# Top-k attention and a cosine FFN on one core: P@V of two units per visit, outputs from ScalarE's queue, decode steps apart, last four units reordered

## The chip, the cores and the metric

The kernel runs on one core of one Trainium2 chip. The metric is the device time of one execution in microseconds (us); lower is better. Before the change the median of 3 runs was 1592.81 us (1592.32 to 1592.93).

A core has five engines with an instruction stream each: TensorE (PE; its weight loads are listed as PEld), VectorE (DVE), ScalarE (ACT), GpSimd (POOL) and SyncE (SP). Each stream runs in order, and an instruction waits for semaphores of other engines or of DMAs. SP only issues DMAs here; a DMA can also be issued from ScalarE's stream.

## The reference

Attention over 8 batches and 8 heads with 576 tokens and 64 dimensions, in which each row keeps its 32 largest scores, followed by a feed-forward network (FFN) over the 4608 tokens:

```python
scores = scale * np.matmul(q, k.transpose(0, 1, 3, 2))
kth = np.partition(scores, -32, axis=-1)[..., -32:-31]
scores = np.where(scores >= kth, scores, -1000000000.0)
scores = scores - np.max(scores, axis=-1, keepdims=True)
attn = np.exp(scores)
attn = attn / (np.sum(attn, axis=-1, keepdims=True) + 1e-09)
x = np.matmul(attn, v)        # then (B,H,S,D) -> (4608, 512)
h = x @ w_in                  # 512 -> 2048
out = (h * np.cos(h)) @ w_out # 2048 -> 512
```

q, k and v are float32. The two weights come as float64 and are read as pairs of 32-bit words; the kernel decodes them to float32.

## The kernel before

**Units and slots.** A unit is 128 tokens of one pair of heads (`hp`); there are 144 units, four for each of 36 blocks of 128 tokens. A loop runs over slots i = 0 to 144. In slot i VectorE does the top-k of unit i: four rounds (`topk_round`, tk0 to tk3) of MAX8 on both heads and, but for the last, MATCH_REPLACE. ScalarE does the mask and the exponentials of unit i-1 (`bounds`, `mask`, `exponentials`; called w). Of unit i-2 (x) VectorE takes the reciprocal of the sums, and GpSimd normalises (`normalise`), splits the words into 16-bit halves (`split`), and SP writes these to DRAM (`write_halves`). For unit i-3 (y) SP issues a transposing DMA that brings the probabilities back as `pT` (`transposes`). For unit i-4 (z) TensorE multiplies `pT` by v (`values`, P@V), and ScalarE copies the result to the block's `xT` (`take_values`). TensorE also computes the scores of unit i+1 in slot i, into the only PSUM tile `sc`, and ScalarE copies them to `s` (`take_scores`). The first eight slots (`early_slot`) and the last four units take a shorter way: TensorE itself transposes (`transposes_now`).

**FFN.** A block with all four units done gets 8 pieces of FF1 (`ff1`, line 380: x @ w_in into PSUM `mm`) and 8 of FF2 (`ff2`, line 456). Between them, per half block (a tile `g` of 1024 columns), ScalarE copies out of PSUM (`take_first`, called by `take_banks`), GpSimd reduces the argument (`reduce_first`, `reduce_second`), ScalarE takes the sine (`sines`, line 437; the sine and the exponential need different tables, so each change costs an ACT_TABLE_LOAD), and GpSimd multiplies (`gate`). The calls `feed(n)` issue up to n pieces; a credit of 4.1 pieces per slot is given out, `ff["tick"]` counts the feeds, and FF2 of a half waits two ticks after its gate. `take_second` copies an output block to `ob` and has SP send it (line 467). After the last slot a loop issues what is left.

**Weights.** 32 chunks of 128 x 512 are loaded in the first slots and decoded in three steps, each on its own engine: `decode_first` (ScalarE, lines 126 to 128), `decode_second` (VectorE, two TENSOR_SCALAR, lines 137 and 138), `decode_third` (GpSimd, two TENSOR_TENSOR, lines 147 and 148). `CHUNKS` bounds the staged chunks and live `g` tiles together.

**Order.** The program fixes the order on every engine: it is that in which the functions `early_slot` and `slot` call the others. SP's stream holds the loads of q, k and v for later batches (`at_slot`), the writes, the transposing DMAs and the outputs, in that order too.

Of the kernel before, what the change touches and what calls it, by code (L numbers as in the profile page):

```python
# [10 lines left out]
F32 = mybir.dt.float32  # L11
# [6 lines left out]
P = 128  # L18
# [13 lines left out]
def kernel(  # L32
# [9 lines left out]
    nc = tc.nc  # L42
# [3 lines left out]
    NT = S // P  # L46
# [83 lines left out]

    def decode_second():


        while wq["second"]:
# [8 lines left out]
    def decode_third(n):  # L143
        for _ in range(min(n, len(wq["third"]))):
            st, w = wq["third"].pop()
# [28 lines left out]
    def load_qk(b, hp):  # L174
        st = pairs.setdefault((b, hp), {})
        also = nc.sync if (b, hp) > (0, 0) else nc.scalar
        t = st["q"] = loads.tile([P, S], F32, tag="q", name="q")
        nc.sync.dma_start(out=t, in_=qT[b, 2 * hp : 2 * hp + 2].rearrange("h d s -> (h d) s"))

        t = st["k"] = loads.tile([P, S], F32, tag="k", name="k")  # L180
        also.dma_start(out=t[0:D], in_=kT[b, 2 * hp])
        nc.sync.dma_start(out=t[D:P, TAIL:S], in_=kT[b, 2 * hp + 1, :, 0:MAIN])
        also.dma_start(out=t[D:P, 0:TAIL], in_=kT[b, 2 * hp + 1, :, MAIN:S])

    def load_v(b, hp):
        st = pairs.setdefault((b, hp), {})
        cols = slice(hp * P, (hp + 1) * P)
        t = loads.tile([P, NT, P], F32, tag="v", name="v", bufs=5)
        nc.sync.dma_start(out=t, in_=v[b, 0:MAIN, cols].rearrange("(c p) e -> p c e", p=P))
# [104 lines left out]
    def transposes(u):  # L294
        rows = u.pop("rows").rearrange("q h k -> (q h) k")
        pT = u["pT"] = work.tile([P, 2 * NT + 1, P], F32, tag="pT", name="pT")
        words = pT.rearrange("p c q -> p (c q)").bitcast(U16)
        nc.sync.dma_start_transpose(
            out=words.rearrange("p (c q) -> p c q", c=2 * NT + 1), in_=rows
        )  # L300

    def transposes_now(u):
# [8 lines left out]
        pT = u["pT"] = work.tile([P, 2 * NT + 1, P], F32, tag="pT", name="pT")  # L311
        for j in range(2):
# [5 lines left out]

    def values(u):

        pT = u.pop("pT")
        o = u["o"] = ps.tile([P, 512], F32, tag="mm", name="o", bufs=4)
        for b, _, rows, r0 in u["parts"]:
            st = pairs[b, u["hp"]]
            r = slice(r0, r0 + rows)
            for c in range(NT + 1):
                for j in range(2):
                    d = slice(j * D, (j + 1) * D)
                    if c < NT:
                        lhsT, rhs = st["v"][:, c, d], pT[:, j * (NT + 1) + c, r]  # L330
                    else:
                        lhsT, rhs = st["v_tail"][:, d], pT[:, NT, r]
                    nc.tensor.matmul(o[d, r], lhsT, rhs, start=c == 0, stop=c == NT)  # L333

    def take_values(u):
        blk = block_of[u["tok"]]
        if "xT" not in blk:
            blk["xT"] = work.tile([P, NP, blk["w"]], F32, tag="xT", name="xT", bufs=5)
        at = u["tok"] - blk["t0"]
        nc.scalar.copy(out=blk["xT"][:, u["hp"], at : at + P], in_=u.pop("o")[:, 0:P])  # L340
        blk["left"] -= 1

# [168 lines left out]
    order = [(b, hp) for b in range(B) for hp in range(NP)]  # L511
    for load, bufs, behind in ((load_qk, 5, -1), (load_v, 5, 4)):
        for n in range(NP, len(order)):
            slot = last[order[n - bufs]] + behind if n >= bufs else NP + 2
            at_slot.setdefault(slot, []).append((load, *order[n]))

# [9 lines left out]
    def early_slot(i, u, w):  # L526
        n = 3 if i < 6 else 2
        if i > 0:
            decode_second()
        topk_round(u, 0)  # L530
        scores(units[i + 1])
        for load, b, hp in at_slot.get(i, []):
            load(b, hp)
        load_weights(n)
        if w:
# [3 lines left out]
            reciprocal(w)  # L539
        topk_round(u, 1)  # L540
        topk_round(u, 2)
        if i == 0:
            decode_second()
        topk_round(u, 3)
        decode_third(1)
        if w:
# [3 lines left out]
        gate(1)  # L550
        decode_third(2)
        feed(2)
# [8 lines left out]
        if w:  # L561
            values(w)
            take_values(w)
        feed(2)
        sines(2)

    def slot(i, u, w, x, y, z):
        now = w and i - 1 >= LAST
        decode_second()
        if x:  # L570
            reciprocal(x)
        if u:
            topk_round(u, 0)
        if w:
            bounds(w)
            mask(w)
            exponentials(w)
        if u:
            topk_round(u, 1)
            topk_round(u, 2)  # L580
        if now:
            reciprocal(w)
        if u:
            topk_round(u, 3)
# [20 lines left out]
        take_banks()  # L605
        decode_third(2)
        decode_first(2)
        if now:
            normalise(w)
        reduce_first()  # L610
        reduce_second()
        feed(2)
        if now:
            transposes_now(w)
            values(w)
            take_values(w)
        feed(1)
        sines(2)

    tt = ps.tile([P, 512], F32, tag="mm", name="warm", bufs=4)  # L620
    for _ in range(8):
        nc.tensor.transpose(tt[:, 0:P], ident, ident)
    load_qk(0, 0)
    load_weights(1)
    load_qk(0, 1)
    load_weights(2)
    scores(units[0])
    take_scores(units[0])
    decode_first(3)
    for i in range(NU + 1):  # L630
# [4 lines left out]
        u, w = (units[i - n] if 0 <= i - n < NU else None for n in range(2))  # L635
        x, y, z = (units[i - n] if EARLY <= i - n < LAST else None for n in range(2, 5))
        if i <= EARLY:
            early_slot(i, u, w)
        else:
            slot(i, u, w, x, y, z)  # L640
    while first or second or full:
# [46 lines left out]
```

## Time and profile before

| | |
|---|---|
| median of 3 runs | 1592.81 us |
| profiled execution: its own time | 1585.37 us |
| profiled execution: span of the instructions | 1583.5 us |
| TensorE busy | 1448.9 us (92%) |
| VectorE busy | 1461.5 us (92%) |
| ScalarE busy | 1155.6 us (73%) |
| GpSimd busy | 1101.0 us (70%) |
| mean share of the DMA engines, queue of SP | 48.6% |
| granted TensorE clock, mean | 0.97 |

All rows below come from one profiled execution. Times are microseconds from the start of its span. Busy time is a union, so two overlapping matmuls count once. In a timeline the number behind the start is how long the group of equal instructions took, and a bracket gives the idle time of the engine before it and what ended that. A wait for several semaphores is put down to the one that came last. A share of busy time over the whole span mixes stages, so the rows are taken stage by stage.

### The profile page before, as it was taken

The page shows a single profiled execution, that of the slowest core. Times are in us where ns is not written, and L with a number is a line of the kernel's source. Part 1 is how long each engine was busy: PE and PEld are TensorE (multiplying, and loading weights), DVE is VectorE, ACT ScalarE, POOL GpSimd, SP SyncE. Part 2 cuts the span into 40 slices and gives each one's busy share as a digit, 9 for nine tenths or more (in the row PEclk, how much of TensorE's full clock was granted, in tenths as well). Part 3 has the DMA queues.
Part 4 walks back from the last instruction along what each step waited for, and adds up shares of the span by engine and source line. Part 5 has one row for each costly group of instructions (what it writes and reads, how often), then busy time and mean ns, then how long its engine had stood idle before and what let it go on. Part 6 is the DMA issues. An engine that isn't in the chain of part 4 may idle for free.

```text
span 1583.5 us, 28533 instructions
## 1 busy us (share of the span) xinstructions
PE 1448.9 (92%) x10356; PEld 1024.1 (65%) x10356; DVE 1461.5 (92%) x3103; ACT 1155.6 (73%) x2244; POOL 1101.0 (70%) x837
## 2 busy tenths in 40 slices
PE   4578778999999999999999999999999999999799
PEld 2466365666666666666666666766666666666575
DVE  7999999999999999999999999999999999999621
ACT  6888756777777777777777777777777777777631
POOL 4688856677777777777777777777777777777500
PEclk9688898999999999999999999999999999999999
DMA  8421454545664456644564446554665446644100
GB/s 270 147 72 51 125 157 133 144 127 151 162 158 127 127 142 165 164 127 141 165 164 127 127 133 174 156 136 125 165 166 134 130 121 155 163 128 130 47 7 14
DMA packets 371596, 212.09 MB, mean 134 GB/s; under 512 B 321280, under 2 KB 337664, under 8 KB 371456
## 3 DMA queue, kind: packets, MB, share of 16 engines
q1 hardware_dynamic: 371296, 210.12, 48.6%
q8 instruction: 81, 1.33, 0.3%
q14 instruction: 59, 0.48, 0.1%
q10 hardware_dynamic: 160, 0.16, 0.0%
HBM read 45.09 MB, written 87.29 MB: 84 GB/s over the span
## 4 chain that ended last, share of the span: by engine, by line
PE 66%; ACT 18%; DVE 9%; DMA 3%; SPq 1%; issue 1%; POOL 0%; ACTq 0%; POOLq 0%; DVEq 0%
PE mm L380 29%; PE o L456 19%; PE o L333 9%; PE sc L206 8%; DVE m L230 4%; DVE rest L233 3%; ACT s L261 3%; DMA pT<-rows 3%; ACT s L253 3%; ACT L437 2%; ACT L261 2%; ACT x L437 2%; ACT s L216 2%; ACT ob L465 1%; ACT nd L244 1%
## 5 line engine op out<-in xcount | busy, mean ns | idle before, releaser
L380 PEld LDWEIGHTS mm<-xT,w_in 128*128 128x128 f32 x4608 | 546.2, 193 | 130.7 <-issue 91.8
L230 DVE MAX8 m<-rest 128x8 f32<-128x576 f32 x864 | 609.6, 747 | 0.0
L380 PE MATMUL mm<-xT,w_in 128*128 128x128 f32 x4608 | 572.3, 279 | 33.1 <-ACT xT L340 33.1
L456 PE MATMUL o<-w_out,g 128*128 128x512 f32 x1152 | 535.9, 598 | 7.3 <-POOL w_out L148 7.0
L233 DVE MATCH_REPLACE8 rest<-m,rest 128x576 f32<-128x576 f32 x576 | 423.6, 743 | 0.0
L287 POOL COPY halves<-s 128x2304 uint16<-128x2304 uint16 x132 | 277.5, 2102 | 176.7 <-DMA rows<-halves 172.3
L456 PEld LDWEIGHTS o<-w_out,g 128*128 128x128 f32 x1152 | 203.3, 191 | 198.5 <-issue 187.9
L275 POOL TENSOR_SCALAR s<-s,rden 128x576 f32<-128x576 f32 x288 | 211.8, 747 | 44.3 <-DVE rden L270 44.1
L230 DVE MAX8 m<-s 128x8 f32<-128x576 f32 x288 | 203.2, 747 | 39.7 <-ACT s L216 39.6
L261 ACT ACTIVATE s<-s,nd 128x576 f32<-128x576 f32 x288 | 219.7, 764 | 0.8
L333 PEld LDWEIGHTS o<-pT,v 128*64 128x64 f32 x2560 | 136.9, 141 | 123.1 <-ACT s L253 42.6
L216 ACT COPY s<-sc 128x1152 f32<-128x1152 f32 x144 | 161.4, 1121 | 71.4 <-PE sc L206 70.5
L233 DVE MATCH_REPLACE8 rest<-m,s 128x576 f32<-128x576 f32 x288 | 211.7, 743 | 0.0
L333 PE MATMUL o<-pT,v 128*64 128x128 f32 (+1 forms) x2560 | 173.3, 276 | 37.4 <-DMA pT<-rows 27.2
L253 ACT ACTIVATE s<-s,nb 128x576 f32<-128x576 f32 x288 | 205.3, 760 | 0.0
L392 ACT ACTIVATE g<-mm 128x512 f32<-128x512 f32 x144 | 85.6, 596 | 159.1 <-PE mm L380 158.9
L206 PE MATMUL sc<-k,q 64*128 64x288 f32 (+1 forms) x1280 | 188.9, 443 | 10.1 <-ACT s L216 6.1
L444 POOL TENSOR_TENSOR g<-g,x 128x1024 f32<-128x1024 f32 x67 | 158.9, 2372 | 14.8 <-ACT x L437 14.8
L427 POOL TENSOR_TENSOR x<-g,x 128x1024 f32<-128x1024 f32 x68 | 161.2, 2370 | 5.7
L418 POOL TENSOR_SCALAR x<-g 128x1024 f32<-128x1024 f32 x68 | 71.3, 1049 | 128.5 <-ACT g L392 119.5
L206 PEld LDWEIGHTS sc<-k,q 64*128 64x128 f32 (+1 forms) x1280 | 102.1, 183 | 54.7 <-issue 20.5
L340 ACT COPY xT<-o 128x128 f32<-128x128 f32 x144 | 37.2, 258 | 100.7 <-PE o L333 100.7
(48 smaller groups left out, 1078.7 us busy)
## 6 DMA issues: line engine op xcount, KB each, us to landing
rows<-halves SPq DMA_DIRECT2D x132, 576.0 KB, 3.3
q<-in_q_dram SPq DMA_DIRECT2D x32, 288.0 KB, 3.2
out_dram<-ob SPq DMA_DIRECT2D x36, 256.0 KB, 2.3
st<-in_moe_w_in_dram SPq DMA_DIRECT2D x16, 512.0 KB, 6.3
v<-in_v_dram SPq DMA_DIRECT2D x32, 256.0 KB, 2.9
st<-in_moe_w_out_dram SPq DMA_DIRECT2D x16, 512.0 KB, 3.5
k<-in_k_dram SPq DMA_DIRECT2D x31, 144.0 KB, 3.4
k<-in_k_dram SPq DMA_DIRECT2D x32, 128.0 KB, 3.6
```

Source lines behind the costliest of these rows:

```text
L206: nc.tensor.matmul(sc[r0 : r0 + rows, j, h, 0:HS], st["q"][d, q0 : q0 + rows], st["k"][d, h * HS : (h + 1) * HS], start=True, stop=True,)
L216: nc.scalar.copy(out=s.rearrange("p j (h w) -> p (j h) w", h=2), in_=u.pop("sc").rearrange("p j h w -> p (j h) w")[:, :, 0:HS],)
L230: nc.vector.max(m8[:, j, at], src[:, j])
L233: nc.vector.match_replace(rest[:, j], m8[:, j, at], src[:, j], NEG)
L253: nc.scalar.activation(out=s[:, j], in_=s[:, j], func=AF.Prelu, bias=nb[:, j, 1:2], scale=SCALE, alpha=FAR)
L261: nc.scalar.activation(out=s[:, j], in_=s[:, j], func=AF.Exp, bias=nd[:, j : j + 1], scale=1.0, accum_out=den[:, j : j + 1],)
L275: nc.gpsimd.tensor_scalar(out=s[:, j], in0=s[:, j], scalar1=rden[:, j : j + 1], scalar2=1.0, op0=ALU.mult, op1=ALU.mult,)
L287: nc.gpsimd.tensor_copy(out=halves, in_=s.rearrange("p (k h) -> p h k", h=2))
L333: nc.tensor.matmul(o[d, r], lhsT, rhs, start=c == 0, stop=c == NT)
L380: nc.tensor.matmul(mm[:, at : at + w], w_in[f // FC][:, c, (f % FC) * P : (f % FC + 1) * P], blk["xT"][:, c], start=c == 0, stop=c == NC - 1,)
L427: nc.gpsimd.tensor_tensor(out=x, in0=g, in1=x, op=ALU.subtract)
L456: nc.tensor.matmul(o, g[:, at : at + P], w_out[f], start=f == 0, stop=f == NF - 1)
```

## The change

P@V: `values` and `take_values` now take a list of units. In odd slots the units i-5 and i-4 are multiplied one after the other into one PSUM bank, and one copy of 128 x 256 takes both to `xT`; in even slots there is no P@V. To hold the older unit a slot longer, `pT` has 3 buffers (2 before) and v has 6 (5 before); `CHUNKS` falls from 9 to 8. FF1 of a block may begin only two ticks after its last copy. The output DMA is issued from ScalarE's stream. `decode_second` stands behind the first top-k round and takes a number; `decode_third` takes all that is ready, behind `normalise`. The last four units get their own function. At the start the loads of q and k of the first unit are split differently.

```diff
-    CHUNKS, XB = 9, 4
+    CHUNKS, XB = 8, 4
...
     def load_qk(b, hp):
...
+        also = nc.sync
+        if (b, hp) == (0, 0):
+            also = nc.scalar
+            also.dma_start(out=q[:, 0:P], in_=qs[:, 0:P])
+        else:
+            nc.sync.dma_start(out=q, in_=qs)
+        also.dma_start(out=k[0:D], in_=kT[b, 2 * hp])
+        nc.sync.dma_start(out=k[D:P, TAIL:S], in_=kT[b, 2 * hp + 1, :, 0:MAIN])
+        nc.sync.dma_start(out=k[D:P, 0:TAIL], in_=kT[b, 2 * hp + 1, :, MAIN:S])
+        if (b, hp) == (0, 0):
+            nc.sync.dma_start(out=q[:, P:S], in_=qs[:, P:S])
...
-    def take_values(u):
-        blk = block_of[u["tok"]]
+    def take_values(us):
+        blk, hp, n = block_of[us[0]["tok"]], us[0]["hp"], len(us)
...
+        nc.scalar.copy(
+            out=blk["xT"][:, hp : hp + n].rearrange("p h q -> p (h q)"),
+            in_=us[0].pop("o")[:, 0 : n * P],
+        )
+        blk["left"] -= n
+        blk["tick"] = ff["tick"]
...
-        nc.sync.dma_start(out=out[row : row + P, :], in_=ob)
+        nc.scalar.dma_start(out=out[row : row + P, :], in_=ob)
...
-        if blk["left"] or wq["ready"] < (((i + 1) * (256 // blk["w"]) - 1) // FC + 1) * NC:
+        if blk["left"] or ff["tick"] < blk["tick"] + 2 or wq["ready"] < (((i + 1) * (256 // blk["w"]) - 1) // FC + 1) * NC:
...
     def early_slot(i, u, w):
         n = 3 if i < 6 else 2
-        if i > 0:
-            decode_second()
         topk_round(u, 0)
+        decode_second(1 if i == 0 else n)
         scores(units[i + 1])
...
     def slot(i, u, w, x, y, z):
-        now = w and i - 1 >= LAST
-        decode_second()
         if x:
             reciprocal(x)
         if u:
             topk_round(u, 0)
+            decode_second(2)
...
-        decode_third(2)
+        decode_third()
         decode_first(2)
-        if now:
-            normalise(w)
         reduce_first()
         reduce_second()
+        feed(3)
+        sines(2)
+
+    def last_slot(i, u, w, x, y, z):
+        if x:
+            reciprocal(x)
+        if u:
+            topk_round(u, 0)
+            topk_round(u, 1)
+        bounds(w)
+        mask(w)
+        exponentials(w)
+        take_banks()
+        sines(1)
+        if z:
+            values(z)
...
+        reciprocal(w)
+        normalise(w)
+        if u:
+            topk_round(u, 2)
+            topk_round(u, 3)
+        gate(2)
         feed(2)
-        if now:
-            transposes_now(w)
-            values(w)
-            take_values(w)
+        transposes_now(w)
+        take_banks()
+        reduce_first()
+        reduce_second()
         feed(1)
-        sines(2)
+        values([w])
+        take_values([w])
+        feed(2)
...
-        x, y, z = (units[i - n] if EARLY <= i - n < LAST else None for n in range(2, 5))
+        x, y = (units[i - n] if EARLY <= i - n < LAST else None for n in range(2, 4))
+        z = units[i - 5 : i - 3] if i % 2 and EARLY <= i - 5 < LAST else None
```

**TensorE's order, slot 83.** Here a block is complete and FF1 of it begins. The names: `o<-pT,v` is P@V, `sc` the scores, `w_in` marks FF1 and `w_out` FF2; the numbers behind `v_tail` belong to the head pairs. Before:

```order
L456 MATMUL o_7179<-w_out_104,g 128x512
L456 MATMUL o_7179<-w_out_105,g 128x512
L333 MATMUL o<-pT,v 64x128 x8
L333 MATMUL o<-pT,v_tail_112 64x128 x2
L206 MATMUL sc<-k,q 128x288 x4
L380 MATMUL mm<-xT,w_in_86 128x128 x16
```

In the changed kernel, at the same place:

```order
L469 MATMUL o_7111<-w_out_104,g 128x512
L469 MATMUL o_7111<-w_out_105,g 128x512
L343 MATMUL o<-pT,v 64x128 x8
L343 MATMUL o<-pT,v_tail_110 64x128 x2
L343 MATMUL o<-pT,v 64x128 x8
L343 MATMUL o<-pT,v_tail_112 64x128 x2
L213 MATMUL sc<-k,q 128x288 x4
L393 MATMUL mm<-xT,w_in_86 128x128 x16
```

Two units' P@V now stand together, and the slot before has none. FF1 of the new block still follows directly on one group of scores.

**ScalarE's order around a sine, an output and a copy of xT.** `x<-x,halfpi` is the sine, `nb`, `nd`, `s` and `den` belong to the exponentials, `ob` is an output block. Before:

```order
L437 ACT_TABLE_LOAD
L437 ACTIVATE x<-x,halfpi 128x1024
L241 ACTIVATE nb<-m_7033 128x4
L244 ACTIVATE nd<-m_7033,nb 128x1 x2
L253 ACTIVATE s<-s,nb 128x576 x2
L261 ACT_TABLE_LOAD
L261 ACTIVATE s,den<-s,nd 128x576 x2
L266 ACTIVATE den<-den,eps 128x2
L465 ACTIVATE ob<-o_6846 128x512
L340 COPY xT<-o 128x128
L216 COPY s<-sc 128x1152
```

In the changed kernel, in the half of the blocks that still have a sine just ahead (the program has 104 table loads in all, 132 before):

```order
L450 ACT_TABLE_LOAD
L450 ACTIVATE x<-x,halfpi 128x1024
L248 ACTIVATE nb<-m_6974 128x4
L251 ACTIVATE nd<-m_6974,nb 128x1 x2
L260 ACTIVATE s<-s,nb 128x576 x2
L268 ACT_TABLE_LOAD
L268 ACTIVATE s,den<-s,nd 128x576 x2
L273 ACTIVATE den<-den,eps 128x2
L478 ACTIVATE ob<-o_6869 128x512
L480 DMA out_dram<-ob 128x512
L349 COPY xT<-o 128x256
L223 COPY s<-sc 128x1152
```

The output's DMA is new in this stream, and the copy of xT is twice as wide. In the other blocks two sines follow one table load a slot after the copy.

**VectorE's order where slots 6 and 7 meet.** `m<-s` is the first MAX8 of a unit, `w_out` the decode. Before:

```order
L137 TENSOR_SCALAR w_out_95<-w_out_95 128x512
L138 TENSOR_SCALAR w_out_95<-w_out_95 128x512
L137 TENSOR_SCALAR w_out_96<-w_out_96 128x512
L138 TENSOR_SCALAR w_out_96<-w_out_96 128x512
L230 MAX m_884<-s 128x8 x2
L233 MATCH_REPLACE rest<-m_884,s 128x576 x2
L270 RECIPROCAL rden<-den 128x2
```

In the changed kernel:

```order
L237 MAX m_881<-s 128x8 x2
L240 MATCH_REPLACE rest<-m_881,s 128x576 x2
L137 TENSOR_SCALAR w_out_94<-w_out_94 128x512
L138 TENSOR_SCALAR w_out_94<-w_out_94 128x512
L137 TENSOR_SCALAR w_out_95<-w_out_95 128x512
L138 TENSOR_SCALAR w_out_95<-w_out_95 128x512
L277 RECIPROCAL rden<-den 128x2
```

The decode of the chunks has moved behind the first round; the reciprocal for which GpSimd's `normalise` waits follows it directly.

## Rows read from the trace of the kernel before

**Rows 1.** The page: busy time of each engine; the chain that ended last.

```profile
PE 1448.9 (92%) x10356; PEld 1024.1 (65%) x10356; DVE 1461.5 (92%) x3103; ACT 1155.6 (73%) x2244; POOL 1101.0 (70%) x837
...
PE 66%; ACT 18%; DVE 9%; DMA 3%; SPq 1%; issue 1%; POOL 0%; ACTq 0%; POOLq 0%; DVEq 0%
```

**Rows 2.** Timeline of VectorE (start, duration, engine, line, instruction, [wait]): first MAX8 of units.

```profile
10.48 0.76 DVE L230 MAX8 m<-s 128x8 f32<-128x576 f32 x1 [9.59 <-ACT s L216]
...
173.96 1.39 DVE L230 MAX8 m<-s 128x8 f32<-128x576 f32 x2
...
283.90 1.40 DVE L230 MAX8 m<-s 128x8 f32<-128x576 f32 x2
...
845.38 1.40 DVE L230 MAX8 m<-s 128x8 f32<-128x576 f32 x2
...
855.09 1.40 DVE L230 MAX8 m<-s 128x8 f32<-128x576 f32 x2
...
1462.26 1.42 DVE L230 MAX8 m<-s 128x8 f32<-128x576 f32 x2 [0.24 <-ACT s L216]
```

**Rows 3.** Timeline of TensorE, one round of four slots.

```profile
853.05 3.17 PE L380 MATMUL mm<-xT,w_in 128*128 128x128 f32 x26 [0.96 <-ACT xT L340]
856.06 1.88 PE L456 MATMUL o<-w_out,g 128*128 128x512 f32 x4
857.78 1.95 PE L380 MATMUL mm<-xT,w_in 128*128 128x128 f32 x16
859.56 1.88 PE L456 MATMUL o<-w_out,g 128*128 128x512 f32 x4
861.37 1.09 PE L333 MATMUL o<-pT,v 128*64 128x128 f32 x16
...
862.62 1.24 PE L206 MATMUL sc<-k,q 64*128 64x288 f32 x8
...
892.74 2.50 PE L380 MATMUL mm<-xT,w_in 128*128 128x128 f32 x20 [0.96 <-ACT xT L340]
```

**Rows 4.** Timeline of ScalarE before the second of these waits.

```profile
884.40 1.28 ACT L437 ACT_TABLE_LOAD   x1
885.69 1.15 ACT L437 ACTIVATE x<-x,halfpi 128x1024 f32<-128x1024 f32 x1
...
892.43 0.26 ACT L340 COPY xT<-o 128x128 f32<-128x128 f32 x1
```

**Rows 5.** Waits of TensorE, whole span: us in total, times, longest.

```profile
PE mm L380 <- ACT xT L340: 33.1, 28, 6.7
PE o L333 <- DMA pT<-rows: 27.2, 14, 7.1
```

**Rows 6.** Timeline of VectorE and GpSimd: decode operations of slots 0 and 1.

```profile
24.12 1.46 POOL L147 TENSOR_TENSOR w_in<-w_in,st 128x512 int32<-128x512 int32 x1
24.36 1.51 DVE L137 TENSOR_SCALAR w_in<-w_in 128x512 f32<-128x512 f32 x1
...
39.77 0.41 DVE L137 TENSOR_SCALAR w_in<-w_in 128x512 f32<-128x512 f32 x1
...
40.56 0.42 DVE L137 TENSOR_SCALAR w_in<-w_in 128x512 f32<-128x512 f32 x1
```

**Rows 7.** Windows: VectorE busy (instructions), line 137, then line 138.

```profile
10.00:174.00 164.00, 19.37 (x32) 0.83 0.42 132
...
10.00:174.00 164.00, 25.18 (x32) 0.83 0.42 132
```

**Rows 8.** Windows: PE, PEld, DVE, ACT, POOL busy, PEclk, DMA share, GB/s.

```profile
0.00:20.00 20.00, 11.13 (x32) 6.76 (x32) 9.57 (x23) 10.04 (x14) 1.87 (x14) 1.00 0.86 242
```

**Rows 9.** Waits of SP's queue, whole span.

```profile
SPq L467 <- ACT xT L340: 227.9, 31, 17.4
```

**Rows 10.** Timeline of ScalarE's queue at the start.

```profile
1.31 0.61 ACTq L183 DMA_DIRECT2D k<-in_k_dram  x1
```

**Rows 11.** Windows: the tail, columns as in rows 8.

```profile
1460.00:1584.00 124.00, 109.72 (x656) 75.69 (x654) 46.36 (x81) 47.78 (x90) 25.47 (x21) 0.97 0.10 29
```

More of the change, by code (lines that the diff above doesn't have):

```diff
@@ L129, in decode_first, with decode_second @@
             wq["second"].append((st, w))
-    def decode_second():
-        while wq["second"]:
+    def decode_second(n):
+        for _ in range(min(n, len(wq["second"]))):
             st, w = wq["second"].popleft()
@@ L141, in decode_second, with decode_third @@
             wq["third"].append((st, w))
-    def decode_third(n):
-        for _ in range(min(n, len(wq["third"]))):
-            st, w = wq["third"].pop()
+    def decode_third():
+        while wq["third"]:
+            st, w = wq["third"].popleft()
             wi = w.bitcast(I32)
@@ L175, in load_qk @@
         st = pairs.setdefault((b, hp), {})
[L176 to L183, printed above, removed]
+        q = st["q"] = loads.tile([P, S], F32, tag="q", name="q")
+        k = st["k"] = loads.tile([P, S], F32, tag="k", name="k")
+        qs = qT[b, 2 * hp : 2 * hp + 2].rearrange("h d s -> (h d) s")
+        also = nc.sync
[9 more added lines that the diff above has]
+            nc.sync.dma_start(out=q[:, P:S], in_=qs[:, P:S])
     def load_v(b, hp):
@@ L187, in load_v @@
         cols = slice(hp * P, (hp + 1) * P)
-        t = loads.tile([P, NT, P], F32, tag="v", name="v", bufs=5)
+        t = loads.tile([P, NT, P], F32, tag="v", name="v", bufs=6)
         nc.sync.dma_start(out=t, in_=v[b, 0:MAIN, cols].rearrange("(c p) e -> p c e", p=P))
@@ L310, in transposes_now @@
             nc.tensor.transpose(to, s[:, c * P : (c + 1) * P], ident)
-        pT = u["pT"] = work.tile([P, 2 * NT + 1, P], F32, tag="pT", name="pT")
+        pT = u["pT"] = work.tile([P, 2 * NT + 1, P], F32, tag="pT", name="pT", bufs=3)
         for j in range(2):
@@ L317, in transposes_now, with values @@
         nc.scalar.copy(out=pT[:, NT], in_=tt[:, 0:P])
[L319 to L333, printed above, removed]
-    def take_values(u):
-        blk = block_of[u["tok"]]
-        if "xT" not in blk:
[L338 to L341, printed above, removed]
+    def values(us):
+        o = us[0]["o"] = ps.tile([P, 512], F32, tag="mm", name="o", bufs=4)
+        for i, u in enumerate(us):
+            pT = u.pop("pT")
+            for b, _, rows, r0 in u["parts"]:
+                st = pairs[b, u["hp"]]
+                r = slice(r0, r0 + rows)
+                to = slice(i * P + r0, i * P + r0 + rows)
+                for c in range(NT + 1):
+                    for j in range(2):
+                        d = slice(j * D, (j + 1) * D)
+                        if c < NT:
+                            lhsT, rhs = st["v"][:, c, d], pT[:, j * (NT + 1) + c, r]
+                        else:
+                            lhsT, rhs = st["v_tail"][:, d], pT[:, NT, r]
+                        nc.tensor.matmul(o[d, to], lhsT, rhs, start=c == 0, stop=c == NT)
+    def take_values(us):
+        blk, hp, n = block_of[us[0]["tok"]], us[0]["hp"], len(us)
+        if "xT" not in blk:
+            blk["xT"] = work.tile([P, NP, P], F32, tag="xT", name="xT", bufs=5)
+        nc.scalar.copy(
[4 more added lines that the diff above has]
+        blk["tick"] = ff["tick"]
     widths = [P] * (B * S // P)
@@ L511 @@
     order = [(b, hp) for b in range(B) for hp in range(NP)]
[L512 to L515, printed above, removed]
+    for n in range(NP, len(order)):
+        i = last[order[n - 5]] - 1 if n >= 5 else 0
+        at_slot.setdefault(max(i, NP + 2), []).append((load_qk, *order[n]))
+        i = last[order[n - 6]] if n >= 6 else 0
+        at_slot.setdefault(max(i + 5 - i % 2, NP + 2), []).append((load_v, *order[n]))
     for hp in range(NP):
@@ L605, in slot @@
         take_banks()
-        decode_third(2)
+        decode_third()
         decode_first(2)
-        if now:
-            normalise(w)
         reduce_first()
         reduce_second()
+        feed(3)
[13 more added lines that the diff above has]
+            values(z)
+        if i + 1 < NU:
+            scores(units[i + 1])
+        if z:
+            take_values(z)
+        if i + 1 < NU:
+            take_scores(units[i + 1])
+        if y:
+            transposes(y)
+        if x:
+            normalise(x)
+            split(x)
+            write_halves(x)
+        reciprocal(w)
[4 more added lines that the diff above has]
+        gate(2)
         feed(2)
-        if now:
-            transposes_now(w)
-            values(w)
-            take_values(w)
+        transposes_now(w)
+        take_banks()
+        reduce_first()
+        reduce_second()
         feed(1)
-        sines(2)
+        values([w])
+        take_values([w])
+        feed(2)
     tt = ps.tile([P, 512], F32, tag="mm", name="warm", bufs=4)
-    for _ in range(8):
+    for _ in range(12):
         nc.tensor.transpose(tt[:, 0:P], ident, ident)
     load_qk(0, 0)
-    load_weights(1)
     load_qk(0, 1)
-    load_weights(2)
+    load_weights(3)
     scores(units[0])
```

13 lines of the change are left out of this document (6 added, 7 removed).

## The prediction

> **What bounds the kernel now.** I read the page first: VectorE and TensorE are both busy 92% of the span and the chain that ended last is 66% TensorE [rows 1]. Two engines that full, in one pipeline, mean that the stage decides, so I next read the start of each unit's first MAX8 on VectorE: it marks the slots. The profile falls into four stages by these rows [rows 2]: the start (to 10.48), twelve slots with decode work (10.48 to 173.96), eleven slots in which the FFN comes up to speed (173.96 to 283.90), 118 steady slots (283.90 to 1462.26), and a tail of 121.2 to the end at 1583.5.
>
> In the steady stage a slot takes (1462.26 - 283.90) / 118 = 9.986 us. A slot in which VectorE never waits takes 855.09 - 845.38 = 9.71; I use 9.70 [rows 2]. So VectorE loses 0.28 per slot, 33.8 in all. TensorE's timeline shows to whom [rows 3]: the first FF1 group of a block starts at 853.05 and again at 892.74, 39.69 apart for four units, and both times it has waited 0.96 for xT. Without that wait TensorE's own work in four units is 38.73, against 4 x 9.70 = 38.80 on VectorE. TensorE is the bound by a hair, and only through that wait. ScalarE's timeline shows why xT is late [rows 4]: the table load for the sines at 884.40, the sine, the exponentials with a table load back, all stand ahead of the copy at 892.43, and FF1 follows at 892.74. The waits table sums it: 33.1 us over 28 waits, and 27.2 over 14 for the DMA transposes [rows 5].
>
> In the decode stage VectorE does not wait for anyone worth naming, it is slow itself. A chunk's two decode operations take 40.56 - 39.77 = 0.79 when GpSimd is still; the same operation took 1.51 beside a GpSimd tensor operation of 1.46 [rows 6]. 32 chunks cost 19.37 + 25.18 = 44.55 [rows 7] where 32 x 0.79 = 25.3 would do: 19.2 us of collision, all in slots that VectorE bounds.
>
> **The change part by part.** The sum is made against the profiled execution (1585.37, span 1583.50); the median of the runs shown, 1592.81, lies 7.44 above it, and I carry that over.
>
> Start: unit 0's scores need 128 columns of q and all of k. Now the first q piece (64 of 288 KB) goes ahead of k on ScalarE's queue, and k's second half leads SP's queue. That is 224 KB less ahead of the last k piece. At some 242 GB/s, what the first 20 us moved [rows 8], 224 KB is 0.9. Taken: -1.0; bounds -2.5 and 0. Four more warm-up transposes run while TensorE has no data.
>
> Decode steps apart: VectorE's decode of chunks moves from the slot's start to after the first top-k round, and GpSimd's part stands behind `normalise`, which waits for the reciprocal that VectorE issues behind its decode. So while VectorE decodes, GpSimd has nothing it may start, if it has finished the slot before. In slots 1 to 5 it has. It has not in slots with `reduce_first`, `reduce_second` or a `split`, and in slot 0 the third chunk meets GpSimd's work on the second. I leave 6 of the 19.2 for these. Against it stand ScalarE's waits: its three decode operations per chunk did not get fewer, the exponentials of unit 0 cannot start before the weights of slot 0 have been decoded, so a slot cannot shrink below ScalarE's own round; I charge 2. The ring of staged chunks is one shorter (8); the weight loads still stand in the same slots, so I cost that at nothing; if a load had to wait, ScalarE would wait for `st`. Taken: -11; bounds -19 (no collision left) and +3 (all stays and the waits are added).
>
> The Trainium skill (SBUF — State Buffer, "Who interferes with whom") says that a two-port VectorE operation and a GpSimd operation lock each other out for a whole instruction. The trace agrees where it shows it: 1.51 beside 1.46, not some share of 0.41. By that rule each decode operation that still meets GpSimd loses the whole overlap, 1.1 in that row (1.51 - 0.41); one such meeting in each of the 13 decode slots would be 14 us, and the decode term -3 instead of -11.
>
> Slots 12 to 22 took 109.9; 11 x 9.70 = 106.7, plus one slot's decode (2 chunks, 1.6) that now falls into it: 108.3. Taken: -2; bounds -3 and +3.
>
> Steady stage. Four edits meet here. (1) FF1 of a new block may be issued only two `feed` calls after its copy, but the order shows it still directly behind the next scores; what changes is ScalarE in front of it: table loads fall from 132 to 104 because two sines more often share a visit, 144 copies of xT become 66 copies of twice the width and 12 single ones. At 1.28 per load [rows 4] the loads alone free 36 us of ScalarE, and every second block's copy has no sine and no table load before it. (2) A pair of units is multiplied per visit: 20 matmuls take 862.62 - 861.37 = 1.25, and the FF2 group before them 1.81 instead of 1.72 [rows 3], so each visit saved is worth 0.09: 0.2 per four units, on an engine whose margin is 0.07. (3) The output DMA leaves SP's queue, where SP waited 227.9 us in 31 places for what ScalarE had to finish [rows 9] with the next transpose behind it; and the older unit of a pair has its transpose one slot longer. I let the steady part of the 27.2 go. (4) ScalarE pays for issuing 36 outputs: a DMA issue on its queue took 0.61 [rows 10], 22 us in all, less than the 36 it was given. What is late next is VectorE itself: 118 x 9.70 = 1144.6 against 1178.4, -33.8. But TensorE's margin is 0.1 to 0.3 in 38.8, and the work between two scores is now uneven, so I allow 0.05 per slot, 6 us. Taken: -28; bounds -34 and, with TensorE still at 39.69 per four units, 0.
>
> On (3) the Trainium skill speaks against the change (DMA: Bandwidth & Descriptors, "Issuing engines are not separate DMA queues"): issuing from another engine saves only the issuing time. By that the output move would be worth nothing here, and the steady stage about 5 us less; the SP row says that the gain lies in the queue's order, not in the transfer.
>
> Tail: TensorE is busy 109.72 of 124 after 1460 [rows 11], so 14 are idle, a few of them the last copy and its DMA. The longest single wait, 6.7 for xT [rows 5], is here. Now the reciprocal of the last four units comes a round earlier, and FF2 pieces stand before each transpose. But fewer FF2 pieces are left behind the last FF1 group (three before its gate is needed, 3 x 1.72 = 5.2, against a chain of copy, two VectorE operations, sine and gate that I estimate to be as long). Taken: -5; bounds -9 and +4.
>
> Sum: -1 - 11 - 2 - 28 - 5 = -47, that is 1538.4 profiled, **1546 us** as median. The bounds together give -67 to +10; the likeliest case alone 1534 to 1560.
>
> **The rivals.** (A) ScalarE takes the place of TensorE's wait: every eighth slot now has both sines after one table load, 1.15 more in one piece, with the scores' copy of the next slot behind it, so VectorE waits there. For it: the copy to `s` and the sines stand in one queue, and in before the copy of xT came 8.0 after the table load [rows 4]. Against it: ScalarE is busy 1155.6 of 1583.5 [rows 1] and gets lighter. Price 1.15 to 2 per eight slots, 17 to 28 over 14.75 such rounds: 1563 to 1574. At its far end TensorE keeps 39.69 and only start, decode and tail gain (19): 1574.
>
> (B) Slower: the pairs make bursts. Between two scores there now stand about 6.5 us of TensorE work and then about 12.4 (1.24 scores, 2.5 values, five FFN pieces of 1.72 or 1.78 [rows 3]). If TensorE cannot run ahead in the short stretch, because the scores' single PSUM tile is not yet copied, the long one exceeds VectorE's 9.70 by 2.7, 59 times: +159. It turns the sum of -47 into a loss from 47 / 59 = 0.8 per pair on. For it: TensorE has no margin to catch up. Against it: the tile is free once ScalarE has copied it, almost a slot before the next scores are due. A third of the full price gives 1546 + 53 = 1599.
>
> (C) The change doesn't do what it says: the xT wait stays, since FF1 of the block still follows directly on one group of scores, and the decode collides elsewhere; start and tail give 6: 1587.
>
> **How the numbers follow.** Forecast 0.64; A 0.21; B 0.08; C 0.04; 0.03 is left for a time below 1534. The median is predicted at 1546, the range 1533 to 1575 takes in A. What can be told from no change is 0.2%, 3.2 us. Faster has forecast, A, most of C and the rest: 0.89; same 0.03; slower 0.08.
>
> **What the profile after would show.** Start of units: slots at 9.70 to 9.75 in the steady stage, the period of four near 38.9; "mm <- xT" below 10 us, "o <- DMA pT" below 10; decode operations summing to about 31 instead of 44.55; output DMAs on ScalarE's queue and none on SP's; the first MAX8 near 9.5; from the last steady slot to the end about 116. The prediction is wrong if VectorE still waits for `s` in the steady stage by more than 0.2 a slot on average (A if a sine precedes the copy, B if TensorE's values do), or if decode still sums to over 40.

## The result, and the profile after

The changed kernel takes 1533.86 us (median of 4 runs, 1532.12 to 1534.66) against 1592.57 us: ratio 0.9633, 95% interval 0.9616 to 0.9650. The forecast was 1546, with a range of 1533 to 1575. The profiled execution took 1532.12 us, span 1530.3.

The page: busy time by engine, and the chain that ended last.

```profile
PE 1430.3 (93%) x10360; PEld 1022.7 (67%) x10360; DVE 1449.0 (95%) x3102; ACT 1109.6 (73%) x2150; POOL 1105.4 (72%) x838
...
DVE 72%; PE 16%; ACT 5%; issue 5%; DMA 1%; POOL 0%; SPq 0%; ACTq 0%; POOLq 0%; DVEq 0%
```

Against [rows 1] the chain has changed sides: 66% TensorE became 72% VectorE. VectorE's timeline shows where (first MAX8 of units 0, 12, 23, 83, 84 and 141, to be held against [rows 2]):

```profile
7.92 0.76 DVE L237 MAX8 m<-s 128x8 f32<-128x576 f32 x1 [7.02 <-ACT s L223]
...
165.63 1.40 DVE L237 MAX8 m<-s 128x8 f32<-128x576 f32 x2
...
275.95 0.74 DVE L237 MAX8 m<-s 128x8 f32<-128x576 f32 x1
...
858.09 1.41 DVE L237 MAX8 m<-s 128x8 f32<-128x576 f32 x2
867.79 0.76 DVE L237 MAX8 m<-s 128x8 f32<-128x576 f32 x1
...
1420.79 0.76 DVE L237 MAX8 m<-s 128x8 f32<-128x576 f32 x1
```

A slot takes 867.79 - 858.09 = 9.70, and so does every one of the steady stage: (1420.79 - 275.95) / 118 = 9.702. The stages, in us:

| | before | after | difference | forecast |
|---|---|---|---|---|
| start, to unit 0 | 10.48 | 7.92 | -2.6 | -1 |
| units 0 to 12 (decode) | 163.48 | 157.71 | -5.8 | -11 |
| units 12 to 23 | 109.94 | 110.32 | +0.4 | -2 |
| units 23 to 141 (steady) | 1178.36 | 1144.84 | -33.5 | -28 |
| tail, unit 141 to the end | 121.2 | 109.5 | -11.7 | -5 |
| span | 1583.5 | 1530.3 | -53.2 | -47 |

The other 5.5 us of the 58.7 between the medians are not in these traces: the profiled execution of before lay 7.2 below this median, that of after 1.7.

TensorE's waits in the whole span (us in total, times, longest), against [rows 5]:

```profile
PE mm L393 <- ACT xT L349: 19.0, 15, 5.8
...
PE o L343 <- DMA pT<-rows: 5.9, 1, 5.9
```

The waits for xT have halved, not vanished; 13 of them, one in every second block, fall into steady slots of 9.70, where they cost nothing. VectorE's decode by windows (lines 137 and 138, as [rows 7]) and the tail (as [rows 11]):

```profile
5.00:183.00 178.00, 16.59 (x32) 0.75 0.45 137
5.00:183.00 178.00, 24.31 (x32) 0.75 0.45 137
```

```profile
1420.00:1531.00 111.00, 104.64 (x634) 69.81 (x632) 42.93 (x79) 45.06 (x85) 26.50 (x22) 0.99 0.09 26
```

The decode still sums to 16.59 + 24.31 = 40.9, above the 40 that the prediction set as a sign of being wrong. In the tail TensorE is idle for 6.4 of 111 us; it was 14 of 124.

### The profile page after: what moved, and what is told of

Read it like the earlier page. It is cut to its first block, busy times and chain, and to the rows that moved or that the text cites. A ratio compares the mean times of both kernels' runs of the same rounds, so it can differ in the third digit from the quotient of the medians.

```text
span 1530.3 us, 28322 instructions
## 1 busy us (share of the span) xinstructions
PE 1430.3 (93%) x10360; PEld 1022.7 (67%) x10360; DVE 1449.0 (95%) x3102; ACT 1109.6 (73%) x2150; POOL 1105.4 (72%) x838
## 3 DMA queue, kind: packets, MB, share of 16 engines
q8 instruction: 81, 1.33, 0.4%
## 4 chain that ended last, share of the span: by engine, by line
DVE 72%; PE 16%; ACT 5%; issue 5%; DMA 1%; POOL 0%; SPq 0%; ACTq 0%; POOLq 0%; DVEq 0%
DVE m L237 36%; DVE rest L240 33%; PE mm L393 6%; PE o L469 6%; PE o L343 2%; PE sc L213 1%; ACT s L268 1%; ACT s L260 1%; DVE w_out L138 1%; ACT st L127 1%; DVE rden L277 1%; DMA v<-in_v_dram 1%; ACT st L128 0%; PE tp L317 0%; DMA st<-in_moe_w_in_dram 0%
## 5 line engine op out<-in xcount | busy, mean ns | idle before, releaser
L343 PEld LDWEIGHTS o<-pT,v 128*64 128x64 f32 x2560 | 136.7, 141 | 69.2 <-issue 37.2
L343 PE MATMUL o<-pT,v 128*64 128x128 f32 (+1 forms) x2560 | 165.7, 272 | 14.3 <-ACT pT L321 8.4
L248 ACT ACTIVATE nb<-m 128x4 f32<-128x4 f32 x144 | 29.6, 206 | 185.3 <-DVE m L237 185.3
```

Of the source, the lines that this page charges most:

```text
L343: nc.tensor.matmul(o[d, to], lhsT, rhs, start=c == 0, stop=c == NT)
```

## Experiments

Two theories of the steady stage stood at the start. Theory Q: the order of queues (outputs ahead of the transposes on SP, work ahead of the copy of xT on ScalarE). Theory W: the TensorE work that pairs save. Each run is compared with the changed kernel's 1533.9 by its median and by the stages of its trace. Medians taken at different times differ by a few us; ratios to the kernel before, timed in turn with it, settle what is close.

**Outputs on SP's queue again.**

```diff
-        nc.scalar.dma_start(out=out[row : row + P, :], in_=ob)
+        nc.sync.dma_start(out=out[row : row + P, :], in_=ob)
```

> The changed kernel with the output DMAs issued from SP's queue again. Theory Q (order of queues: the steady slots came down because nothing stands in front of the transposing DMAs on SP and less in front of the copy of xT on ScalarE): the waits of P@V for pT come back, 5.9 us in the changed kernel and 27.2 before, so +10 to +20 us over 1533.9, steady slots 9.78 to 9.87. Theory W (work: two units per visit save TensorE about 0.28 us in four slots, and this slack absorbs small waits): within +3 us, steady slots stay at 9.70.

1535.7 us, ratio 0.9651 (0.9634 to 0.9669), not told apart from the changed kernel; steady slots 9.702, no wait for pT in the steady stage. Theory Q misses: with pairs and the two ticks the output's queue is worth nothing that can be told.

**One unit of P@V per slot.**

```diff
-        z = units[i - 5 : i - 3] if i % 2 and EARLY <= i - 5 < LAST else None
+        z = [units[i - 4]] if EARLY <= i - 4 < LAST else None
```

> The changed kernel with one unit of P@V per slot again (unit i-4), copies of xT of 128 x 128, all else as changed (3 buffers of pT, outputs on ScalarE's queue, two ticks before FF1). Theory Q: the work saved by pairs is small and the queue in front of the transposes stays clear, 0 to +5 us over 1533.9. Theory W: TensorE gets its work back, 10.1 us by the two profiles (P@V 238.9 before, 228.8 after), and with it the lack of slack: +10 to +25 us, steady slots 9.78 to 9.9, and waits for xT in nearly every block (28 before, 15 in the changed kernel).

1542.9 us, ratio 0.9707 (0.9687 to 0.9728), +9: between the two, so it decides nothing alone. Steady slots 9.764, the steady waits are 12.0 us for pT in 10 places and none for xT. That last zero speaks against W.

**Both undone.** The two diffs above together.

> The changed kernel with both undone: one unit of P@V per slot and outputs on SP's queue. If the two edits add up: the sum of what each costs alone. Theory Q: nearly all of the steady gain of 33 us is lost, +20 to +33. Theory W: as with single units alone, +10 to +25. If either edit alone already holds the slots at VectorE's 9.70, each alone shows about 0 and only this one shows the loss.

1575.0 us, ratio 0.9905 (0.9877 to 0.9934), +41: 2 and 9 do not add up to it. So each of the two edits alone nearly holds the slots at VectorE's 9.70, and only without both is the loss there. Here is one such place; first SP's queue, then TensorE, then TensorE's windows (busy, granted clock, DMA share, GB/s):

```profile
927.40 0.33 SPq L480 DMA_DIRECT2D out_dram<-ob  x1
927.78 0.42 SPq L185 DMA_DIRECT2D q<-in_q_dram  x1
...
930.05 2.72 SPq L305 DMA_TRANSPOSE pT<-rows  x1
```

```profile
934.99 1.85 PE L343 MATMUL o<-pT,v 128*64 128x128 f32 x16 [2.23 <-DMA pT<-rows]
936.61 0.65 PE L343 MATMUL o<-pT,v_tail 128*64 128x128 f32 x4
```

```profile
932.00:935.00 3.00, 0.77 (x9) 1.00 1.22 289
935.00:938.50 3.50, 3.50 (x32) 0.52 0.19 72
938.50:942.00 3.50, 3.50 (x23) 0.99 0.48 135
```

The output and a head pair's loads stand ahead of the transpose, the transpose comes late, and TensorE waits 2.23. Then it is paid once more: the granted clock is 0.52, about the lower level of 1.2 GHz, for the 3.5 us behind the wait, and the 16 matmuls take 1.85 where [rows 3] have 1.09. The slots there took 10.77 and 11.28 by VectorE's timeline. Not every wait is followed by this. Eight of the 18 waits for pT in the steady stage are; behind one of 2.16 that ended at 817.4 us the clock stayed at 1.00:

```profile
817.40:821.00 3.60, 3.60 (x38) 1.00 0.42 119
```

**No two ticks before FF1.**

```diff
-        if blk["left"] or ff["tick"] < blk["tick"] + 2 or wq["ready"] < ...
+        if blk["left"] or wq["ready"] < ...
```

> The changed kernel without the condition that FF1 of a block waits two ticks after its last copy. Theories Q and W: FF1 still follows behind the next scores, 0 within 2 us. Theory D (the delay itself takes the wait for xT away): the waits for xT double from 19 us and +5 to +15 us.

1559.5 us, ratio 0.9805 (0.9785 to 0.9825): +25.6, a surprise to Q and W. Theory D has the sign and the waits, too small a time: the steady waits for xT nearly double, to 23.3 us in 28 places. Steady slots are at 9.824 (14 us of the 25.6), the tail is 117.3 (8 us), and the table loads are 134 instead of 104: it is the two ticks that make the sines share a visit.

**The kernel before with outputs from ScalarE's queue alone.** The same line as in the first diff, turned round.

> The kernel before with the one edit that outputs are issued from ScalarE's queue. Theory Q: the waits for pT go from 27.2 to below 10 us and the time to 1575 to 1582. Theory W: TensorE stays at 39.69 us in four slots, since the wait for xT takes over: within 3 us of 1592.6.

1604.2 us, ratio 1.0084 (1.0059 to 1.0109): the edit alone makes the kernel slower, which no theory had. Steady slots 10.18; 37.6 us of waits for xT in 25 places, against 23.7 in 25 before in the same slots.

**The kernel before with pairs alone.** Built from the changed kernel by taking back the outputs, the two ticks, the decode order and the last four units; the start stays new.

> The kernel before with pairs alone: two units of P@V per visit (with their buffers, 8 staged chunks and the loads of the start that go with the new kernel), outputs on SP's queue, decode order and last four units as before, no two ticks. Theory Q: the pairs alone leave SP's queue as it was, though a unit's transpose has a slot more: 1570 to 1580. Theory W: the pairs carry the steady gain: 1545 to 1560.

1544.8 us, ratio 0.9718 (0.9702 to 0.9733). Steady slots 9.702: pairs alone bring the whole steady gain.

The last three runs are read together on ScalarE and TensorE. First the run without the two ticks, at the start of a block:

```profile
915.37 0.58 ACT L478 ACTIVATE ob<-o 128x512 f32<-128x512 f32 x1
915.98 0.34 ACTq L480 DMA_DIRECT2D out_dram<-ob  x1
916.36 0.37 ACT L349 COPY xT<-o 128x256 f32<-128x256 f32 x1 [0.41 <-ACT ob L478]
...
916.78 3.39 PE L393 MATMUL mm<-xT,w_in 128*128 128x128 f32 x28 [1.04 <-ACT xT L349]
```

The same place with pairs alone, outputs on SP:

```profile
904.33 0.58 ACT L478 ACTIVATE ob<-o 128x512 f32<-128x512 f32 x1
904.80 0.36 ACT L349 COPY xT<-o 128x256 f32<-128x256 f32 x1
...
900.63 1.09 PE L343 MATMUL o<-pT,v 128*64 128x128 f32 x16
...
905.22 3.39 PE L393 MATMUL mm<-xT,w_in 128*128 128x128 f32 x28 [0.41 <-ACT xT L349]
```

From the start of `ob` to that of xT it is 0.99 in the one and 0.47 in the other. The issue of the output, which waits for `ob` to be complete, puts the copy of xT 0.5 us later, and TensorE's wait grows from 0.41 to 1.04. Theory C grew from this: an output on ScalarE's queue costs half a us in front of FF1, and pairs with two ticks can bear it, pairs alone cannot.

How pairs shorten the wait shows against the kernel before, where the P@V ahead of the second wait of [rows 3] is this:

```profile
888.44 1.09 PE L333 MATMUL o<-pT,v 128*64 128x128 f32 x16
```

There TensorE came to the missing xT at 892.74 - 0.96 = 891.78, 3.3 us after P@V began. With pairs, two units' P@V stand in that place, and it comes at 905.22 - 0.41 = 904.81, 4.2 us after. ScalarE is no faster: from the sine's table load to the copy of xT it is 8.0 us in [rows 4] and 8.2 here (the load starts at 896.59), and both kernels have 132 table loads. So pairs fill TensorE's wait with work of the slot before.

**Outputs on SP and no two ticks, the rest as changed.**

> The changed kernel with outputs on SP's queue and without the two ticks: what is left of the change is pairs, decode order, last four units and start. Theory C (the output's issue puts ScalarE's copy of xT 0.5 us later, and without the two ticks that uses up TensorE's slack): steady slots 9.70 as in before_pairs, waits for xT near 0.4 each, 1531 to 1541 depending on the tail (109 to 117). Rival: the two ticks themselves are what keeps the slots at 9.70 once the other edits are in: 1550 to 1560, as no_two_ticks.

1542.1 us, ratio 0.9707 (0.9687 to 0.9727). Steady slots 9.701, 8.7 us for xT in 22 places: theory C holds for the steady stage. The time is above its range by 1 us; 113.1 of it are the tail, where a wait of 2.5 for xT is back.

**One unit per slot, one slot later, outputs on SP, two ticks kept.**

```diff
-        at_slot.setdefault(max(i + 5 - i % 2, NP + 2), []).append((load_v, *order[n]))
+        at_slot.setdefault(max(i + 5, NP + 2), []).append((load_v, *order[n]))
...
-        z = units[i - 5 : i - 3] if i % 2 and EARLY <= i - 5 < LAST else None
+        z = [units[i - 5]] if EARLY <= i - 5 < LAST else None
```

> The changed kernel with outputs on SP's queue and one unit of P@V per slot, but of unit i-5 instead of i-4: each transposing DMA has one slot more, TensorE's work and ScalarE's 144 copies are as with single units. To be read against single_and_sp (1575.0, steady slots 10.03). Theory L (lateness: with one slot, a transpose that lands late costs TensorE the wait and then matmuls at the lower clock): waits for pT fall from 42.4 to below 12 us, steady slots 9.70 to 9.78, 1536 to 1546. Theory W (work: the 0.28 us in four slots that pairs save decide): steady slots stay at 9.95 to 10.05, 1565 to 1577.

1543.4 us, ratio 0.9707 (0.9688 to 0.9726). Steady slots 9.702, no wait for pT in the steady stage. Theory W falls: TensorE has the same work here as in the run of 1575.0, at 10.03 per slot. What helped there was the slot that the transpose was given. (The tail is 117.8, 8.3 longer than with the change; the same edit in the kernel before, next, makes it 8.6 longer, to 129.8.)

**The kernel before with that one edit.** The same change of `z` in the kernel before, with 3 buffers of pT, 6 of v and 8 staged chunks.

> The kernel before with one edit: P@V of unit i-5 instead of unit i-4, one unit per slot as before (3 buffers of pT, 6 of v, loads of v a slot later, 8 staged chunks); outputs on SP's queue, decode order, start and last four units as before, no two ticks. Theory L (in the kernel before, the one slot that a transpose had was what cost the 33 us, directly by the waits for pT and the lower clock behind them, and through them by the waits for xT): steady slots 9.70 to 9.75, 1548 to 1562. Rival X (the waits for xT before FF1, 33.1 us in 28 places, were the bound by themselves, as the prediction read them): steady slots stay at 9.9 to 10.0, 1575 to 1592.

1585.7 us, ratio 0.9985 (0.9975 to 0.9994). Rival X is right. Waits of TensorE in the steady stage of this run, the whole list:

```profile
PE mm L380 <- ACT xT L340: 30.3, 30, 2.2
```

The waits for pT are gone, and the slots stay at 9.95: the wait for xT, one in each block, holds TensorE at 39.7 us in four slots by itself, as the prediction had read from [rows 3]. All eleven kernels of this question, with the steady slot and TensorE's waits there (us, times):

| P@V | outputs | two ticks | slot | xT | pT |
|---|---|---|---|---|---|
| unit i-4 (before) | SP | no | 9.986 | 23.7, 25 | 10.9, 10 |
| unit i-4 | ACT | no | 10.181 | 37.6, 25 | 12.3, 9 |
| unit i-4 | SP | yes | 10.033 | 0 | 33.2, 18 |
| unit i-4 | ACT | yes | 9.764 | 0 | 12.0, 10 |
| unit i-5 | SP | no | 9.954 | 30.3, 30 | 0 |
| unit i-5 | SP | yes | 9.702 | 7.3, 14 | 0 |
| pairs | SP | no | 9.702 | 8.3, 23 | 2.3, 5 |
| pairs, new tail and decode | SP | no | 9.701 | 8.7, 22 | 2.1, 5 |
| pairs | ACT | no | 9.824 | 23.3, 28 | 2.8, 5 |
| pairs | SP | yes | 9.702 | 11.8, 12 | 0 |
| pairs (after) | ACT | yes | 9.702 | 12.9, 13 | 0 |

There are two obstacles. One is xT late for FF1. The two ticks take these waits away or leave them in every second block at most, and pairs leave 0.4 us in most blocks; neither moves the slots off 9.70. Pairs without the ticks fail only where an output stands in front of the copy (9.824). The other is pT late for P@V. A slot more removes it, which pairs give the older unit too; outputs off SP's queue lessen it only beside the two ticks (33.2 to 12.0; without them 10.9 and 12.3). Both have to go for VectorE to set the slot. The change has pairs against both, the two ticks against the first and the output move against the second.

**The last four units in the order of before.** `last_slot` with the order of the old `slot`: reciprocal behind the third top-k round, `normalise` behind `feed(2)`, transposes and values behind the next `feed(2)`.

> The changed kernel with the last four units in the order of before. Theory: the tail came down from 121.2 to 109.5 us by this edit: its single wait for xT of 6.7 us goes, and less work is left at the last unit: +8 to +12 us over 1533.9. Rival: the tail is shorter because the steady slots leave TensorE less in arrears, whatever the order of the last four: +0 to +4.

1545.0 us, ratio 0.9722 (0.9701 to 0.9744), +11; tail 119.4. TensorE's waits after 1419 and its window there:

```profile
PE mm L393 <- ACT xT L349: 6.4, 1, 6.4
PE o L343 <- ACT pT L321: 2.7, 4, 0.7
```

```profile
1419.00:1539.00 120.00, 106.44 (x628) 71.86 (x627) 43.45 (x79) 42.38 (x83) 23.59 (x20) 0.97 0.08 24
```

The wait of 6.4 is the one of 6.7 of before, and idle time is 13.6 of 120 again. So 9.9 of the tail's 11.7 are this edit's. Without the two ticks less of it is left: the tail is 113.1 (outputs on SP) or 117.3 with the same edit.

**Decode steps in the order of before.**

```diff
     def early_slot(i, u, w):
...
+        if i > 0:
+            decode_second(99)
         topk_round(u, 0)
-        decode_second(1 if i == 0 else n)
...
     def slot(i, u, w, x, y, z):
+        decode_second(99)
...
             topk_round(u, 0)
-            decode_second(2)
...
-        decode_third()
+        decode_third(2)
```

`decode_third(n)` takes the newest n chunks, and `early_slot` also calls it with 1 before `normalise`, as before. There are 8 staged chunks; with 9 the pool would need 56 KB per partition, and 52.8 are left.

> The changed kernel with the decode steps in the order of before (VectorE's at the slot's start, GpSimd's two per slot, newest first), 8 staged chunks. Theory: the two profiles put the gain of the decode stage at 5.4 us (268.0 against 273.4 from the first unit to unit 23), so +3 to +6 us over 1533.9, decode operations of VectorE summing to about 44 instead of 40.9. Rival: the decode order was worth the 11 us forecast and another edit took 6 of them back: +9 to +12. Second rival: it is worth nothing: 0 within 2.

1531.7 us, ratio 0.9640 (0.9624 to 0.9657): no difference from the changed kernel. By the medians it would be 2 us faster, by the ratios 0.1% slower, so it isn't a better version either. The second rival holds. Units 0 to 23 took 268.1, as with the change. The windows of the decode, lines 137 and 138:

```profile
5.00:183.00 178.00, 21.41 (x32) 0.74 0.46 137
5.00:183.00 178.00, 22.52 (x32) 0.74 0.46 137
```

43.9 against 40.9: between these two traces the new order has 3.0 us less of VectorE's decode. It gives them back. VectorE's waits for the sums of ScalarE between 21 and 180 us, first with the changed kernel, then here:

```profile
DVE rden L277 <- ACT den L273: 4.9, 4, 2.1
```

```profile
DVE rden L277 <- ACT den L273: 1.7, 1, 1.7
```

3.2 us more of waiting with the new order, for 3.0 us less of decode. But even the 3.0 are not the order's in every trace. Eight kernels here have the new order and GpSimd's reduction: four sum to 40.9 or 41.0, the other four (outputs on SP, the two without the two ticks, one unit a slot later) to 43.7 to 44.0, and their units 0 to 23 take 266.9 to 273.8 us. The five with the old order sum to 43.6 to 44.8 and take 268.1 to 273.4.

**Reduction of the early slots on VectorE.**

```diff
-        if ff["end"]:
+        if ff["end"] or ff["now"] <= 13:

             nc.vector.tensor_scalar(
...
-        if not ff["end"]:
+        dve = ff["end"] or ff["now"] <= 13
+        if not dve:
             nc.gpsimd.tensor_tensor(out=x, in0=g, in1=x, op=ALU.subtract)
```

> The changed kernel with the FFN's reduction of slots up to 12 on VectorE (two operations of 0.69 and 1.23 us) instead of GpSimd (four, 5.5 us). Theory E (in slots 7 to 12 a slot is GpSimd's work plus VectorE's decode, since the two do not overlap: 12.2 + 1.7 = 13.9, measured 13.8): the collisions go, decode sums to 26 to 30 us instead of 40.9, and slots 7 to 12 take 12.0 to 13.3, so -4 to -10 us. Rival: the collision is hidden behind ScalarE, whose work sets the slot: decode falls but the time stays within 3 us, or rises by the 1.9 us per reduction.

1535.6 us, ratio 0.9664 (0.9648 to 0.9680). The rival's time: it stays, though not shown to be because ScalarE sets the slot. The collisions go in slots 7 and 8 (4.2 to 1.7 each), but decode still sums to 37.2, above what theory E expected: in slots 9 to 12 VectorE now meets GpSimd's gate, split and decode steps instead, and pays 1.9 for each reduction. Slots 7 to 12 took 82.3 us, 80.5 with the change.

## Why the prediction was right

The sign, the range and the place of the gain were right: the steady stage decides, TensorE's wait for xT was the bound there, and VectorE's own 9.70 is what comes next. The time lies 0.14 us below the likeliest case's own lower end of 1534, and luck has a part in the sum: decode and units 12 to 23 brought 7.6 us less than forecast, and start, steady stage and tail 13.8 more. Of the prediction's own signs, the slots, the waits for pT and the outputs' queue came true; the waits for xT (19.0, not below 10) and the decode sum (40.9, not 31) did not, and over 40 was named as a sign that it is wrong. Of the 12.1 us between 1546.0 and 1533.9, 6.2 are in the terms, and 5.7 come from carrying over the 7.44 between the profiled execution and the median of before, of which after had only 1.7.

- **Steady, -28: -33.5.** The allowance of 0.05 per slot was not needed; slots are at 9.702. That the wait for xT was the bound is shown by the run with P@V a slot later: it is the only wait left there, and its 30.3 us are the 118 x (9.954 - 9.702) = 29.7 that the slots lose. The reasons given for its end were not the right ones. Edit (1): a last copy of a block that has a sine ahead still makes TensorE wait (13 of 15 times), the other does not; but the freed table loads are not needed, since pairs alone with 132 loads and the run with outputs on SP and no ticks with 134 are at 9.70 too. Edit (2): nor is the saved work, since single units a slot later hold 9.702 with the two ticks. Pairs alone give all of the gain, by the work that they put in front of FF1 and the slot that they give a transpose.
- **The output move, step (3), was wrong.** It was said that SP's queue order was the gain and that ScalarE pays less than it was given. On the kernel before the edit costs 13 us by its ratio, since its issue stands in front of the copy of xT; with pairs and two ticks it is worth nothing that can be told. Only with single units and two ticks does it pay, 32 us. The Trainium skill (DMA: Bandwidth & Descriptors, "Issuing engines are not separate DMA queues") says that issuing elsewhere saves only the issue. For the changed kernel that was the better forecast; for single units, 1575.0 against 1542.9, the order of the queue counts more than the issue.
- **The two ticks were costed at nothing, wrongly.** FF1 does follow the same scores at the place shown, but without them the changed kernel takes 25.6 us more, and 30 more table loads.
- **Decode, -11: -5.8 in the traces, nothing by the run with the old order. This is the step that failed.** "GpSimd has nothing it may start, if it has finished the slot before" holds in slots 1 to 6, whose decode takes 0.85 per chunk. From slot 7 on it has not finished. Timeline of VectorE and GpSimd of the changed kernel in slot 7:

```profile
101.23 0.90 DVE L137 TENSOR_SCALAR w_out<-w_out 128x512 f32<-128x512 f32 x1
102.17 2.45 DVE L138 TENSOR_SCALAR w_out<-w_out 128x512 int32<-128x512 int32 x1
104.53 0.41 DVE L137 TENSOR_SCALAR w_out<-w_out 128x512 f32<-128x512 f32 x1
```

```profile
100.81 1.04 POOL L433 TENSOR_SCALAR x<-x 128x1024 f32<-128x1024 f32 x1
101.94 2.39 POOL L440 TENSOR_TENSOR x<-g,x 128x1024 f32<-128x1024 f32 x1
```

  VectorE's 0.4 us operation takes 2.45, as long as GpSimd's reduction beside it. 15.6 of the 19.2 us of collision stayed, not 6. The rule of the Trainium skill on the lock (SBUF — State Buffer, "Who interferes with whom") gave -3 for this term in the prediction, nearer to the 0 that the run with the old order shows. Of the 5.4 us by which units 0 to 23 got shorter in these traces, 3.2 are not the decode's at all (next point). The rest, 3.6 less of decode and 1.7 more of waiting for the sums, is less than kernels with one decode order differ by.
- **Units 12 to 23, -2: +0.4.** The plan was 106.7 plus 1.6 for the decode of two chunks in slot 12. That slot took 13.32, 3.6 over 9.70, because these operations collide as well. Here are its first, beside GpSimd's split of 2.10 us, and its last, beside GpSimd's own decode of 1.33:

```profile
168.39 1.47 DVE L137 TENSOR_SCALAR w_out<-w_out 128x512 f32<-128x512 f32 x1
...
170.69 1.39 DVE L138 TENSOR_SCALAR w_out<-w_out 128x512 int32<-128x512 int32 x1
```

  Against it, slots 19 and 20 of the kernel before took 11.13 and 11.47, 3.2 over 9.70 together, where TensorE waited for two transposes (its waits from 230 to 270 us):

```profile
PE o L333 <- DMA pT<-rows: 14.2, 2, 7.1
```

  These waits go with pairs alone and with P@V a slot later alone: units 12 to 23 take 106.7 and 106.6 there, with the old decode order.
- **Tail, -5: -11.7**, outside the bounds of -9 and +4. With the two ticks in place the reorder is worth 9.9 by the tails. The stall feared at the end is not in the trace: TensorE does its last FF2 pieces without a wait.
- **Start, -1: -2.6**, just past the bound. Kernels with the new start began at 7.0 to 7.9, those with the old one at 8.7 to 10.5, so 0.8 to 3.5 us is what can be said.
- **Rivals.** A and B both needed VectorE to wait for `s` in the steady stage; in the changed kernel it never does. C was right that FF1 still waits for xT in many blocks and that the decode collides elsewhere, and wrong that this waiting must cost.

## What to carry to other kernels

When two engines are both nearly full, look for every wait that can put the slower one behind, and test the parts of a change in pairs: here two edits that cost 2 and 9 us when undone alone cost 41 when undone together. A transfer that feeds a full engine was better served here by one more stage of the pipeline (slots of 9.702) than by a better place in its queue (9.764). A DMA issued from an engine that computes waits in order for its data there, so ask which copy stands behind it.

## What was not expected of the hardware

- A late operand can be paid twice on TensorE: after 2.23 us without matmuls, 3.5 us ran at a granted clock of 0.52 (the lower level), in a stretch that is otherwise at 1.00. After a wait of 2.16 elsewhere in the same run it stayed at 1.00.
- Issuing an output of 256 KB from ScalarE's stream took 0.34 us, but delayed the next copy by 0.52, since the issue waits until the operation that fills the block has ended (0.58 us) and the copy starts 0.04 behind the issue.
